# A margin of a moment before a maximum is handed to a busy PSUM bank, in the front of a two-branch attention kernel

## The chip, the cores and the metric

The kernel runs on one core of a Trainium2 chip. The core has five engines that run side by side and meet at semaphores: TensorE (PE, with its weight loader PEld), VectorE (DVE), ScalarE (ACT), GpSimd (POOL) and the queue of SyncE (SP), which issues DMAs. TensorE writes to PSUM banks of 128 x 512 words, and VectorE and ScalarE read them. The metric is the device time of one execution in microseconds; it was 1465.76 us for the kernel before (median of 3 runs, 1465.62 to 1465.98).

## What is computed

One sequence of 2048 rows with 512 columns, x, goes through two attentions, which a gate mixes:

```python
g = sigmoid((x * gate_w).sum(-1))
out = g * A(x) + (1 - g) * B(x)
# A: 32 heads of 16; row i looks at rows i, i-2, ..., i-14 (8 of them, dilated by 2)
# B: 32 heads of 16 queries over ONE head of keys and values
scores = einsum("bhqd,bkd->bhqk", q, k) * 16**-0.5    # 32 x 2048 x 2048
p = softmax(scores); o = einsum("bhqk,bkd->bhqd", p, v)
```

Branch B is the larger one by far: its 32 x 2048 x 2048 scores are made twice, once to find the largest score of each row (the *maxima* below, which the softmax subtracts) and once for the exponentials.

## The kernel before, in words

B's scores are cut in 32 units (4 blocks of 512 queries by 8 groups of 4 heads), each of 16 steps of 128 keys. For the maxima a unit has 64 pieces, one for each of 2 x 2 x 4 blocks of 128 rows and 4 blocks of 512 keys: 2048 in all (`NF`). The pieces are 62 rows deep, so two of them, or one and a piece of other work, run side by side on the upper and the lower half of TensorE's rows. Such a pair of places is called a slot here.

The program is written out by a planner in Python: it keeps a clock for TensorE, ScalarE and VectorE (`clk`), the time at which every PSUM bank is free (`free`), and a list of tasks with due times (`tasks`), and at each slot it decides what the next instructions are. Nothing of that is left at run time: each engine has a fixed order of instructions, and where a bank isn't free yet, the engine waits at its semaphore, with all that is behind it in its queue. The planner counts 0.23 us for a slot (`T_R`), 0.20 for the way from a matmul to its reader (`T_LAT`), 0.66 for a fused add-and-maximum (`T_TTR`), 1.14 and 0.61 for the maximum of a pair and of a single.

There are three stages.

- **The front** (`stream` called with `mm` and `done_mm`, profile lines L1209 for its matmuls): 62 lumps of work, the query projections of B (14) and the query, key and value projections of A (48), each of 12 products that are split in two row halves and add up in the banks `pe`. `stream` hands out one projection matmul per row half and slot. Between them it puts maxima in: in a slot where a maximum goes to one half, the projections go on in the other. In the first part of the front these are whole maxima: `fill_pair` (two matmuls at L387 into bank `pm`, key `m2`; one VectorE reduction at L416) and `fill_one` (one matmul at L387 into `ps` or `po`, keys `m1` and `po`; one reduction at L427).
- In the later part of the front the maxima are taken in *halves*. `half_keys` and `half_parts` form half the sum and half the difference of neighbouring blocks of keys (matmuls at L456 with the matrix `sel`, ScalarE at L464, VectorE at L468, into the tile `kcd`). Then max(a, b) = (a+b)/2 + |a-b|/2: `fill_diff` makes the difference (matmul L483 into a half of `pm`, |.| by ScalarE at L509 into the buffer `dd`), and `fill_sum` the sum (matmul L483 into `ps` for the one row half and `po` for the other, and one VectorE instruction at L526 that adds `dd` and takes the maximum). Two matmuls so give two pieces, but with half of VectorE's work. `diff_ready` and `sum_ready` say whether one may be handed out; `paired` says whether the next two pieces can be taken in halves, among others because the half keys of their blocks are there (`formed`). At most 468 pieces (`FRONT`) are begun in the front in this way.
- **The attention stage** (512 steps): per step two pairs of score matmuls (L571), two exponentials on ScalarE (L573), eight matmuls with the values (L581), and one pair and at times one single of the maxima that are left (L387). Branch A's arithmetic runs beside it on POOL (L645 to L705). Twice an **output phase** (`out_phase`, L865) interrupts it; it calls `stream` too. The list `pe` is empty in the front and not empty from the attention stage on, which is how functions of both tell where they are.

The order around the change is thus set by comparisons of `free[...]` with `clk["pe"]` in `stream`, `sum_ready` and `diff_ready`. Before, a sum, a single or a pair could be handed out when its bank would be free within 0.1 us:

```python
return bool(pend[odd]) and free[("m1", "po")[odd]] <= clk["pe"] + 0.1 and pend[odd][0][2] <= clk["pe"] + 0.4
```

and a difference as soon as its half of `pm` is free. `formed[g]` was set to 0.0 when `half_parts` had been written out.

Of the kernel before, what the change touches and what calls it, by code (L numbers as in the profile page):

```python
# [43 lines left out]
FRONT = 468  # L44
LEAD, M2S, M1S, E1S, PER_ROW = 3.0, 0.5, 0.3, 0.2, 21
M2H = 0.15
WB = 6


# [31 lines left out]
def gated_mix_kernel(ctx, tc, xt, wa, wk, wq, wo_a, wo_b, out):  # L81
# [27 lines left out]
    m1 = pp.tile([P, 512], F32, name="ps")  # L109
    po = pp.tile([P, 512], F32, name="po")  # L110
    m2 = Banks(tc, "pm")

    def split(hi, lo, src, eng=None):
        nc.scalar.activation(hi, src, AF.Copy)
        (eng or nc.vector).tensor_sub(lo, src, hi.bitcast(F32))

    clk = {"pe": 0.0, "act": 0.0, "dve": 0.0}

    def after(eng, ready, dur):
        clk[eng] = max(clk[eng], ready) + dur  # L120
        return clk[eng]
# [15 lines left out]
    raw = [first[:, k, :] for k in range(4)]  # L137
    raw += [p1.tile([P, 512], F32, name="xraw", tag=tag, bufs=WB) for tag in ("wah", "wal") for _ in range(6)]
    xraw = {(t, c): raw[C * t + c] for t in range(NQB) for c in range(C)}
# [16 lines left out]
    def load_wa(gg, c):  # L156
        waraw[gg, c] = p1.tile([P, GN], F32, name="waraw", bufs=2)
        nc.gpsimd.dma_start(waraw[gg, c], wa[c * P:(c + 1) * P, gg * GN:(gg + 1) * GN])

    def split_wa(gg, c):  # L160
        nonlocal pool
        wah[gg, c] = p1.tile([P, GN], F32R, name="wah", bufs=WB)
        wal[gg, c] = p1.tile([P, GN], F32R, name="wal", bufs=WB)
        split(wah[gg, c], wal[gg, c], waraw.pop((gg, c)), nc.gpsimd)
        after("act", clk["pe"], 0.62)
        pool = max(pool, clk["pe"] * 1e3) + 1300

    def ahead_wa(gg, k):

        if 0 <= k < 2 * C and k % 2 == 0:  # L170
            load_wa(gg, k // 2)
        if 2 < k <= (2 * C if gg == 0 else 2 * (WB - C)) + 1 and k % 2:
            split_wa(gg, (k - 3) // 2)
# [188 lines left out]
    slots = [(v, pr, t, kc) for kc in range(2) for v in range(2) for pr in range(2) for t in range(4)]  # L362
# [3 lines left out]
    free = {"m2": 0.0, "m1": 0.0, "e0": 0.0, "e1": 0.0, "po": 0.0}  # L366
# [3 lines left out]
    def fillable():  # L370
        return bool(half) or bool(slots) and slots[0][0] < len(stacked) and stacked[slots[0][0]] <= clk["pe"]
# [17 lines left out]
    def to_go():  # L389
        return 2 * len(slots) + len(half)  # L390
# [41 lines left out]
    sel, kcd, dd, formed, ended, wants = [], [], [], {}, set(), []  # L432
# [15 lines left out]
    def half_keys(g):  # L448

        if g == 0:  # L450
            hb[g] = (m2.shape(2)[:, 0, :], m2[:, 1, :])
        keys = ("m2", "m2") if g == 0 else ("m1", "po")
        clk["pe"] = max(clk["pe"], *(free[k] for k in keys))
        for x in range(2):
            for y in range(2):
                nc.tensor.matmul(hb[g][x], sel[0][:, x * y], kst[:, (2 * g + y) * 512:(2 * g + y + 1) * 512], start=(y == 0), stop=(y == 1))  # L456
        clk["pe"] += 1.2
        for k in keys:
            free[k] = clk["pe"] + 4.0
        tasks.append((clk["pe"] + 1.0, half_parts, (g, keys)))  # L460

    def half_parts(g, keys):
        for x in range(2):
            nc.scalar.activation(kcd[0][:, g, x], hb[g][x], AF.Identity, scale=mk[:, 0:1])  # L464
            at = after("act", clk["pe"], 0.65)
        for x in range(2):
            parts = kcd[0][:, g, x]
            nc.vector.scalar_tensor_tensor(parts, hb[g][x], mk[:, 1:2], parts.bitcast(F32), op0=ALU.mult, op1=ALU.add)  # L468
            free[keys[x]] = after("dve", at + 0.1, 0.7) + 0.1
        tasks.append((clk["dve"] + 1.5, lambda: nc.sync.dma_start(kd[:, g], kcd[0][:, g].bitcast(F32)), ()))  # L470
        formed[g] = 0.0

    def half_back():

# [3 lines left out]
    def paired():  # L478
        return len(slots) > 1 and slots[0][3] % 2 == 0 and formed.get(slots[0][3] // 2, 1e9) <= clk["pe"] and slots[1] == slots[0][:3] + (slots[0][3] + 1,) and fillable()
# [4 lines left out]

    groups, pend, half_free = [], [[], []], [0.0, 0.0]

    def diff_ready(odd):

        if max(half_free) != free["m2"]:
            half_free[:] = [free["m2"]] * 2  # L490
        if half_free[odd] > clk["pe"] or clk["dve"] - 1.6 > clk["pe"]:
            return False
        mine = [g for g in groups if odd in g[2]]
        if not mine and (groups or half or ended or wants or not paired() or not pe and NF - to_go() >= FRONT):
            return False
        d = mine[0][1] if mine else dd[0]
        return all(x[1] is not d for x in pend[odd])

    def fill_diff(odd):
        mine = [g for g in groups if odd in g[2]]  # L500
        if not mine:
            mine = [(slots.pop(0), dd[0], {0, 1})]
            slots.pop(0)
            dd.append(dd.pop(0))
            groups.append(mine[0])
        (v, pr, t, kc), d, todo = mine[0]
        m2.shape(2)
        half_mm(m2[:, odd, :], v, pr, t, kc, 1, odd)
        nc.scalar.activation(d[:, odd], m2[:, odd, :], AF.Abs)  # L509
        half_free[odd] = after("act", clk["pe"] + T_R + T_LAT, 0.54) + 0.1  # L510
        free["m2"] = max(half_free)
        pend[odd].append(((v, pr, t, kc), d, half_free[odd]))
        todo.discard(odd)
        if not todo:
            groups.remove(mine[0])

    def sum_ready(odd):

        return bool(pend[odd]) and free[("m1", "po")[odd]] <= clk["pe"] + 0.1 and pend[odd][0][2] <= clk["pe"] + 0.4

    def fill_sum(odd):
        (v, pr, t, kc), d, ready = pend[odd].pop(0)
        m = unit_tile(v)
        dst, key = ((m1, "m1"), (po, "po"))[odd]
        half_mm(dst, v, pr, t, kc, 0, odd)
        nc.vector.tensor_tensor_reduce(d[:, odd], dst, d[:, odd], 1.0, -FMAX, ALU.add, ALU.max, m[:, odd, pr, t, kc:kc + 1])  # L526
        free[key] = after("dve", max(clk["pe"] + T_R + T_LAT, ready), T_TTR) + 0.08
        filled(v, 2)
# [35 lines left out]
    pe, pexp, exped = [], {}, {}  # L564
# [251 lines left out]
    def stream(seq, mm, done, pooled):  # L816

        at, told = [0, 0], 0
        ended.clear()
        while min(at) < len(seq):  # L820
            lone = {}
            if wants and all(free[k] <= clk["pe"] + 0.1 for k in (("m1", "po") if wants[0] else ("m2",))):
                half_keys(wants.pop(0))
            halves = groups or any(pend) or paired() and not half
            if halves or 1 in wants:
                for b in range(2):
                    if sum_ready(b):
                        lone[b] = lambda b=b: fill_sum(b)
                    elif diff_ready(b):
                        lone[b] = lambda b=b: fill_diff(b)  # L830
                        break
            elif fillable() and free["m1"] <= clk["pe"] + 0.1:
                lone[half[0][4] if half else 0] = lambda: fill_one(m1, "m1")
            elif pooled and fillable() and free["po"] <= clk["pe"] + 0.1:
                lone[half[0][4] if half else 0] = lambda: fill_one(po, "po")
            dur = 0.0
            for b in sorted((0, 1), key=lambda b: b not in lone):
                if b in lone:
                    now = clk["pe"]
                    lone[b]()  # L840
                    clk["pe"] = now
                elif at[b] < len(seq):
                    dur = max(dur, mm(b, seq[at[b]]))
                    at[b] += 1
            after("pe", 0, T_R if lone else dur)
            if not (ended or 0 in wants or halves) and slots and fillable() and free["m2"] <= clk["pe"] + 0.1:
                clk["pe"] = max(clk["pe"], free["m2"])
                fill_pair(m2, "m2")
            while told < min(at):
                told += 1  # L850
                done(seq[told - 1])

    def out_phase(js, n, whole_unit):
# [40 lines left out]
        while groups or any(pend):  # L894
            for b in range(2):
                if sum_ready(b):
                    fill_sum(b)
                elif diff_ready(b):
                    fill_diff(b)
            clk["pe"] += T_R  # L900
# [311 lines left out]
    def done_mm(at):  # L1212
        nonlocal pool
        x, i = at
        lump = lumps[x]
        if lump[0] == "a" and lump[2] == NJ - 1 and lump[1] + 1 < GG and i in (2, 5) and WB - C < 4:
            c = WB - C + (i == 5)
            if c < C:
# [175 lines left out]
```

## Time and profile before

| what | value |
|---|---|
| median of the runs | 1465.76 us |
| the profiled execution | 1465.73 us |
| its span, first to last instruction | 1463.9 us |
| granted TensorE clock | 1.000 |
| busy PE / PEld / DVE / ACT / POOL | 1454.2 / 676.5 / 1191.3 / 1286.7 / 1002.8 us |
| front, first to last projection (L1209) | 26.3 to 268 us |
| first and last difference or sum in the front (L483) | 97.6 and 262.4 us |

In the profile a line as L483 is a line of the kernel; `ps<-kcd,qst` means that the tile `ps` is written from `kcd` and `qst`; x20 counts instructions. PEld is the weight loader, which works ahead of the matmuls, so that an idle time of PEld isn't in full an idle time of the array. Ends of matmuls are modelled, and matmuls overlap, so the busy time of PE doesn't tell how many of them went through; the starts do. A wait is given as "who waited <- what ended it: us in total, times, longest".

### The profile page before, as it was taken

The numbers are of one execution on the slowest core, as the hardware profiler recorded it, in microseconds if no ns is written. First come the engines' busy times: TensorE is split into PE (matmuls) and PEld (weight loads), VectorE is DVE, ScalarE is ACT, GpSimd is POOL, SyncE is SP. The second block draws the span as 40 slices with busy tenths as digits, with TensorE's granted clock in tenths as the row PEclk, the third lists the DMA queues.
The fourth block names the chain that finished last, engine by engine and source line by source line (L and its number), as shares of the span: only waits on it lengthen the run. The fifth ranks groups of instructions, "written<-read, shape, count | busy, mean of one in ns | idle before, by whom it ended". The sixth has DMA issues, their size and how long they took to land.

```text
span 1463.9 us, 29004 instructions
## 1 busy us (share of the span) xinstructions
PE 1454.2 (99%) x10612; PEld 676.5 (46%) x10612; DVE 1191.3 (81%) x1867; ACT 1286.7 (88%) x1629; POOL 1002.8 (69%) x1753
## 2 busy tenths in 40 slices
PE   9999999999999999999999999999999999999998
PEld 5877777533333333333333476333333364333343
DVE  6978889688888888888888888888888888888712
ACT  5658888899999999999999988999999988999986
POOL 7853889778898988988878898798988341011221
PEclk9999999999999999999999999999999999999999
DMA  6753433222121120211202111121120000000110
GB/s 225 210 162 77 147 90 103 74 56 66 42 86 34 54 79 22 71 42 42 72 20 74 42 60 60 42 71 38 46 70 14 12 27 16 12 1 2 29 32 30
DMA packets 75263, 89.80 MB, mean 61 GB/s; under 512 B 56368, under 2 KB 56416, under 8 KB 70896
## 3 DMA queue, kind: packets, MB, share of 16 engines
q1 hardware_dynamic: 68176, 49.00, 11.9%
q0 software_dynamic: 6368, 37.90, 7.7%
q8 instruction: 83, 1.36, 0.4%
q10 hardware_dynamic: 576, 1.05, 0.2%
q14 instruction: 60, 0.49, 0.1%
HBM read 60.03 MB, written 27.35 MB: 60 GB/s over the span
## 4 chain that ended last, share of the span: by engine, by line
PE 96%; DVE 2%; POOL 1%; DMA 1%; issue 0%; ACT 0%; DVEq 0%; POOLq 0%; ACTq 0%
PE po L581 34%; PE pe L571 23%; PE pe L1209 10%; PE pm L387 8%; PE ps L387 6%; PE pe L865 4%; PE pm L483 3%; PE ps L483 2%; PE po L483 2%; PE pm L936 1%; PE pe L211 1%; DVE mx L416 1%; DMA xraw<-xt 1%; DVE mx L427 0%; POOL qlo L257 0%
## 5 line engine op out<-in xcount | busy, mean ns | idle before, releaser
L573 ACT ACTIVATE pexp<-pe 128x1024 f32<-128x1024 f32 x1022 | 987.9, 1023 | 83.2 <-PE pe L571 78.7
L416 DVE TENSOR_REDUCE mx<-pm 128x2 f32<-128x1024 f32 x504 | 617.3, 1225 | 145.2 <-PE pm L387 141.7
L581 PE MATMUL po<-pexp,vst 128*32 128x512 f32 x4096 | 545.5, 605 | 0.8 <-DVE tt L595 0.8
L571 PE MATMUL pe<-qst,kst 64*128 64x512 f32 x1916 | 442.8, 451 | 0.0
L571 PEld LDWEIGHTS pe<-qst,kst 64*128 64x128 f32 x1916 | 180.0, 183 | 473.4 <-ACT pexp L573 466.7
L427 DVE TENSOR_REDUCE mx<-ps 128x1 f32<-128x512 f32 x402 | 273.8, 681 | 0.7 <-PE ps L387 0.7
L387 PE MATMUL pm<-kst,qst 62*128 62x512 f32 x973 | 196.9, 397 | 0.7 <-ACT pexp L573 0.4
L645 POOL TENSOR_TENSOR pr<-aext 128x256 f32<-128x256 f32 x256 | 182.6, 741 | 4.6 <-DMA aext<-ad 4.3
L705 POOL TENSOR_TENSOR oa<-oa,av 128x256 f32<-128x256 f32 x224 | 164.3, 733 | 15.1
L581 PEld LDWEIGHTS po<-pexp,vst 128*32 128x32 f32 x4096 | 80.6, 108 | 168.0 <-issue 158.6
L387 PE MATMUL ps<-kst,qst 62*128 62x512 f32 x394 | 155.5, 395 | 0.2 <-DVE mx L427 0.2
L702 POOL TENSOR_TENSOR av<-aext,lg 128x256 f32<-128x256 f32 x224 | 139.6, 623 | 12.7
L509 ACT ACTIVATE dd<-pm 128x512 f32<-128x512 f32 x182 | 102.4, 605 | 21.1 <-PE pm L483 11.8
L1209 PE MATMUL pe<-wah,xh 64*128 64x512 f32 x376 | 119.2, 397 | 0.0
L1209 PE MATMUL pe<-wah,xl 64*128 64x512 f32 x376 | 118.5, 395 | 0.0
L1209 PE MATMUL pe<-wal,xh 64*128 64x512 f32 x376 | 117.5, 394 | 0.0
L387 PEld LDWEIGHTS pm<-kst,qst 62*128 62x128 f32 x973 | 94.5, 186 | 4.5 <-DVE mx L416 1.6
L651 POOL TENSOR_TENSOR tr<-pr 128x512 f32<-128x512 f32 x64 | 81.7, 1277 | 4.3
L509 ACT ACTIVATE pexp<-pm 128x512 f32<-128x512 f32 x124 | 70.5, 606 | 13.2 <-PE pm L483 8.3
L608 POOL TENSOR_TENSOR rl<-rl,gate_t 128x16 f32<-128x16 f32 x31 | 6.9, 223 | 107.2 <-DVE rl L602 99.7
L651 POOL TENSOR_TENSOR tr<-tr 128x256 f32<-128x256 f32 (+1 forms) x128 | 72.5, 567 | 8.6
L387 PEld LDWEIGHTS ps<-kst,qst 62*128 62x128 f32 x394 | 73.6, 187 | 4.2 <-DVE mx L427 1.1
(215 smaller groups left out, 1972.6 us busy)
## 6 DMA issues: line engine op xcount, KB each, us to landing
aext<-ad POOLq DMA_DIRECT2D x32, 1056.0 KB, 5.6
qst<-qd SPq DMA_DIRECT2D x60, 128.0 KB
ad<-stage SPq DMA_DIRECT2D x32, 240.0 KB
xraw<-xt SPq DMA_DIRECT2D x16, 256.0 KB
qd<-qhi SPq DMA_DIRECT2D x16, 256.0 KB
qd<-qlo SPq DMA_DIRECT2D x16, 256.0 KB
qst<-qd SPq DMA_DIRECT2D x60, 64.0 KB
qst<-ml SPq DMA_DIRECT2D x216, 2.0 KB
```

What stands on the lines that cost most here:

```text
L387: nc.tensor.matmul(dst, qst[home(v)[0]][b:b + 62, pr, t * P:(t + 1) * P], kst[b:b + 62, kc * 512:(kc + 1) * 512], start=True, stop=True)
L416: nc.vector.tensor_reduce(m[:, :, pr, t, kc], dst, AX.X, ALU.max)
L427: nc.vector.tensor_reduce(m[:, odd, pr, t, kc:kc + 1], dst, AX.X, ALU.max)
L509: nc.scalar.activation(d[:, odd], m2[:, odd, :], AF.Abs)
L571: nc.tensor.matmul(bank[:, odd, :], kst[b:b + 64, kt * P:(kt + 1) * P], qst[home(u)[0]][b:b + 64, pr, :], start=True, stop=True)
L573: nc.scalar.activation(e, bank, AF.Exp, scale=SCALE)
L581: nc.tensor.matmul(po[32 * i:32 * i + 32, :], vst[:, kt, :], pexp[s, i // 2][:, i % 2, :], start=(kt == 0), stop=(kt == NJ - 1))
L645: nc.gpsimd.tensor_mul(pr[:, k], q, e[:, o:o + NH, AC:2 * AC])
L651: nc.gpsimd.tensor_add(nx, cur[:, :, 0:n], cur[:, :, n:2 * n])
L702: nc.gpsimd.tensor_mul(av, e[:, o:o + NH, 2 * AC:].rearrange("p j (h d) -> p j h d", d=DH), lg[:, w].unsqueeze(3).to_broadcast([P, NH, AG, ...
L705: nc.gpsimd.tensor_add(ao, ao, av)
L1209: nc.tensor.matmul(front[2 if x == last else x % 2][0][:, b, :], l[h], r[h], start=(i == 0), stop=(i == 3 * C - 1))
```

## The change

Three comparisons of the front and one due time are altered; no instruction is added or taken out, only the order in which the planner writes them.

A constant `JUST` of 0.05 us and a function `just()` come in, which is 0.05 in the front and -0.1 from the attention stage on. Where a maximum was handed out with its bank free within the next 0.1 us, the front now asks that the plan has had the bank free for 0.05 us: in `sum_ready`, for `fill_one` on `ps` and `po`, and for `fill_pair` on `pm`. `diff_ready` asks for 0.05 instead of 0. In the output phases all four stay as they were, since -0.1 gives the old margin (and 0 in `diff_ready`). And `formed[g]` is the planner's VectorE clock after the half keys' last instruction, plus 0.1, instead of 0.0.

```diff
+JUST = 0.05
@@ half_parts
-        formed[g] = 0.0
+        formed[g] = clk["dve"] + 0.1
@@
+    def just():
+        return -0.1 if pe else JUST
@@ diff_ready
-        if half_free[odd] > clk["pe"] or clk["dve"] - 1.6 > clk["pe"]:
+        if half_free[odd] > clk["pe"] - max(0.0, just()) or clk["dve"] - 1.6 > clk["pe"]:
             return False
@@ sum_ready
-        return bool(pend[odd]) and free[("m1", "po")[odd]] <= clk["pe"] + 0.1 and pend[odd][0][2] <= clk["pe"] + 0.4
+        return bool(pend[odd]) and free[("m1", "po")[odd]] <= clk["pe"] - just() and pend[odd][0][2] <= clk["pe"] + 0.4
@@ stream
-            elif fillable() and free["m1"] <= clk["pe"] + 0.1:
+            elif fillable() and free["m1"] <= clk["pe"] - just():
                 lone[half[0][4] if half else 0] = lambda: fill_one(m1, "m1")
-            elif pooled and fillable() and free["po"] <= clk["pe"] + 0.1:
+            elif pooled and fillable() and free["po"] <= clk["pe"] - just():
                 lone[half[0][4] if half else 0] = lambda: fill_one(po, "po")
@@ stream
-            if not (ended or 0 in wants or halves) and slots and fillable() and free["m2"] <= clk["pe"] + 0.1:
+            if not (ended or 0 in wants or halves) and slots and fillable() and free["m2"] <= clk["pe"] - just():
                 clk["pe"] = max(clk["pe"], free["m2"])
                 fill_pair(m2, "m2")
```

## The prediction

> **What bounds the kernel now.** I read the shares of the chain first, then the stages, then the waits inside the stage that the change touches.
>
> ```profile
> PE 96%; DVE 2%; POOL 1%; DMA 1%; issue 0%; ACT 0%; DVEq 0%; POOLq 0%; ACTq 0%
> ```
>
> The chain that ended last lies on TensorE for 96% of the span. TensorE takes its matmuls in the written order, so time is won where one of them waits and everything behind it waits too. The profiled execution took 1465.73 us with a span of 1463.9, that is 1.83 outside the span; the median of the runs, 1465.76, is 0.03 above it. A change within 0.2%, 2.9 us, is about what a measurement can't tell from none.
>
> The stages, with one query each: all instructions, then the projections (L1209) alone, then the maxima in halves (L483) alone, each for 108 to 263 us; columns are window, length, and per engine busy time with its instructions.
>
> ```profile
> 30.00:92.50 62.50, 62.30 (x524) 53.88 (x524) 60.67 (x85) 37.01 (x80) 53.21 (x47) 1.00 0.68 189
> 108.00:263.00 155.00, 155.00 (x1270) 114.79 (x1268) 132.44 (x386) 134.34 (x269) 114.52 (x177) 1.00 0.38 106
> 108.00:263.00 155.00, 153.85 (x914) 110.46 (x912) 1.00 0.38 106
> 108.00:263.00 155.00, 117.14 (x356) 62.28 (x356) 1.00 0.38 106
> ```
>
> The front is the stretch up to 268 us; its second part carries 914 projection matmuls and 356 maxima matmuls. Two matmuls run side by side on the two halves of the rows, so 1270 are 635 slots. What an undisturbed slot takes, the order of time shows (start, length):
>
> ```profile
> 61.58 0.42 PE L1209 MATMUL pe<-xh,wqh 64*128 64x512 f32 x2
> 61.81 0.41 PE L1209 MATMUL pe<-xl,wqh 64*128 64x512 f32 x2
> ...
> 62.74 0.41 PE L1209 MATMUL pe<-xl,wqh 64*128 64x512 f32 x2
> 62.98 0.41 PE L1209 MATMUL pe<-xh,wql 64*128 64x512 f32 x2
> ```
>
> From 61.58 to 62.98 are six slots (the rows cut out begin 0.23 or 0.24 apart too), so one is 1.40 / 6 = 0.233 us. 635 x 0.233 = 148.0 of 155 us: at most 7.0 us of this stretch are matmuls that waited, although busy PE reads 155.00 of 155. Who waited:
>
> ```profile
> PEld ps L483 <- DVE mx L526: 9.2, 35, 0.4
> PEld po L483 <- DVE mx L526: 8.5, 36, 0.4
> PEld pm L483 <- ACT dd L509: 2.9, 14, 0.3
> PEld pe L1209 <- DVE stage L317: 0.3, 1, 0.3
> ```
>
> The weight loader waits 71 times, 17.7 us, for VectorE to read a sum's bank (ps or po). The loader runs ahead of the matmuls, so not all of this is lost. One recurrence of bank ps:
>
> ```profile
> 214.44 0.40 PE L483 MATMUL ps<-kcd,qst 62*128 62x512 f32 x1
> 214.91 0.40 PE L1209 MATMUL pe<-wah,xh 64*128 64x512 f32 x1
> 214.99 0.69 DVE L526 CUSTOM_DVE_ANT_0 dd<-ps,dd 128x512 f32<-128x512 f32 x1
> 215.04 0.18 PEld L483 LDWEIGHTS po<-kcd,qst 62*128 62x128 f32 x1 [0.17 <-DVE mx L526]
> 215.15 0.40 PE L483 MATMUL po<-kcd,qst 62*128 62x512 f32 x1
> 215.39 0.39 PE L1209 MATMUL pe<-wah,xh 64*128 64x512 f32 x1
> 215.60 0.08 DVE L526 DVE_READ_ACCUMULATOR2_ANT mx<- 128x1 f32 x1
> 215.74 0.18 PEld L483 LDWEIGHTS ps<-kcd,qst 62*128 62x128 f32 x1 [0.40 <-DVE mx L526]
> 215.74 0.50 PE L483 MATMUL ps<-kcd,qst 62*128 62x512 f32 x1
> 216.08 0.39 PE L1209 MATMUL pe<-wah,xl 64*128 64x512 f32 x1
> ```
>
> The next sum on ps was due at 215.39 + 0.23 = 215.62, began at 215.74, and the slot after it began 0.34 later instead of 0.23: 0.12 + 0.11 = 0.23 us lost, one slot, with a loader's wait of 0.40. The wait of 0.17 at 215.04 cost nothing: po began at 215.15, 0.24 after its neighbour. So some 0.17 of each wait is covered.
>
> **The change, part by part.** *The margin of the sums, from 0.1 us too early to 0.05 us late (sum_ready).* No instruction is added or removed; some are written later. In the plan's numbers a sum's bank is free 0.23 + 0.20 + 0.66 + 0.08 = 1.17 us after its slot begins. With the old margin the next sum may go when 1.07 have passed, which is the fifth slot (5 x 0.23 = 1.15); with the new one 1.22 must pass, which is the sixth (1.38). The trace says that the bank really needs 215.74 - 214.44 = 1.30 us, and six real slots are 1.40. So a quick recurrence, given out one slot too early now and paid with a lost slot, would find its bank free, and the lost slot would carry a projection. The gain from below: 17.7 - 71 x 0.17 = 5.6 us (waits shorter than their cover count against it). From above: the 7.0 us less what the ScalarE waits lose, 2.9 - 14 x 0.17 = 0.5, so 6.5. I take 5.6, the figure from the waits themselves; at 0.23 each these are 24 recurrences.
>
> *The same margin for the first part's maxima (fill_one, fill_pair).* The reductions of a pair and of a single:
>
> ```profile
> L416 DVE TENSOR_REDUCE mx<-pm 128x2 f32<-128x1024 f32 x504 | 617.3, 1225 | 145.2 <-PE pm L387 141.7
> L427 DVE TENSOR_REDUCE mx<-ps 128x1 f32<-128x512 f32 x402 | 273.8, 681 | 0.7 <-PE ps L387 0.7
> ```
>
> In 30 to 92.5 us VectorE is busy 60.67 of 62.50, and that covers a later issue: with three banks in turn, the two others hold a reduction of a pair and one of a single, 1.23 + 0.68 us of VectorE's work (or two singles, 1.36), while a bank is refilled one slot later. Cost nothing; without the cover it would be 0.23 us a round.
>
> *The first group of a half (diff_ready, 0.05 later).* The plan gives ScalarE's read 0.23 + 0.20 + 0.54 + 0.1 = 1.07 us, the fifth slot lies at 1.15 and so 0.08 behind it: the new margin moves little, and I leave the 0.5 us of those waits where they are.
>
> *Half keys ready when VectorE is through.* Now the first such matmul goes as soon as the work on the keys is written down:
>
> ```profile
> 96.47 0.40 PE L1209 MATMUL pe<-wah,xl 64*128 64x512 f32 x2
> 96.65 0.74 DVE L468 SCALAR_TENSOR_TENSOR kcd<-po,mk,kcd 128x512 fp32r<-128x512 f32 x1
> 97.57 0.18 PEld L483 LDWEIGHTS pm<-kcd,qst 62*128 62x128 f32 x1 [1.13 <-issue]
> 97.60 0.47 PE L483 MATMUL pm<-kcd,qst 62*128 62x512 f32 x1 [0.74 <-PE pe L1209]
> ```
>
> It was due at 96.47 + 0.23 = 96.70 and began at 97.60: 0.90 us lost behind the write of the keys at 96.65 to 97.39. Between nothing (the plan's VectorE clock runs ahead) and 0.90; I take 0.90, since the new due time is that very instruction's. A plain maximum of a pair may slip in before the first group and hold it up by its 1.2 us of VectorE; that moves a few maxima and no projection.
>
> *What comes later for it.* The count of projections is fixed, so the front ends 5.6 + 0.9 = 6.5 us sooner and with fewer maxima. They go at 356 / 155 = 2.3 a us, so 6.5 x 2.3 = 15; the 24 recurrences come 0.10 later each, 1.2 us on either bank, 3 more: 18 maxima move to the attention stage. Each spares half a slot in front, 0.117 us, 2.1 in all. What one costs later, units of 16 steps (32 exps, L573) with different counts of maxima show (all engines, then L573 alone, then L387 alone):
>
> ```profile
> 399.90:433.00 33.10, 33.10 (x238) 11.92 (x234) 27.49 (x34) 31.01 (x33) 29.49 (x49) 1.00 0.29 94
> 1245.60:1279.50 33.90, 33.74 (x242) 12.20 (x241) 29.24 (x34) 31.02 (x33) 0.84 (x2) 1.00 0.04 10
> 399.90:433.00 33.10, 30.92 (x32) 1.00 0.29 94
> 399.90:433.00 33.10, 10.00 (x44) 5.08 (x42) 1.00 0.29 94
> 433.00:466.40 33.40, 11.02 (x47) 5.46 (x45) 1.00 0.05 14
> 1245.60:1279.50 33.90, 11.61 (x48) 5.68 (x47) 1.00 0.04 10
> ```
>
> 0.8 us for four maxima more is 0.20 each, 0.3 for three is 0.10. The floor is nothing (ScalarE, 31.0 of 33 to 34 us, hides it), the ceiling far off a whole matmul's length, 0.395. I take 0.15, between the two pairs: 18 x 0.15 = 2.7. The attention stage's own margins stay as they are. POOL's branch A sets when the second output phase may start:
>
> ```profile
> 1149.74 0.73 POOL L705 TENSOR_TENSOR oa<-oa,av 128x256 f32<-128x256 f32 x1
> 1171.24 0.24 POOL L533 TENSOR_TENSOR mh<-mt,mk 128x32 fp32r<-128x32 f32 x1 [20.67 <-DVE mt L406]
> ```
>
> It is done 20.67 us ahead of the next work on POOL, more than the front can shrink, so that phase keeps its unit; if it didn't, it would begin 34 us later.
>
> **Sum:** -5.6 - 0.9 - 2.1 + 2.7 = -5.9 us. Against the profiled 1465.73 that is 1459.8.
>
> **The rivals.** *A, the forecast:* 1459.8, with its own range from 1456.2 (6.5 + 0.9 + 2.1 and nothing later: 9.5) to 1462.8, where 2.9 is won.
>
> *B, the front isn't paced by TensorE.* In 108 to 263 us ScalarE is busy 134.34 and VectorE 132.44 of 155 us, the weight loader only 114.79. If ScalarE paces, each slot won turns into a wait of a projection for its bank, and only the half keys' 0.9 stays: 1464.8. Against it:
>
> ```profile
> L509 ACT ACTIVATE dd<-pm 128x512 f32<-128x512 f32 x178 | 100.1, 606 | 19.4 <-PE pm L483 10.1 <-PE pe L1209 5.9 <-PE ps L483 2.2
> ```
>
> ScalarE idles 19.4 us ahead of the half maxima, 18.2 of it for TensorE: it follows. The Trainium skill, "Perfetto Trace Analysis", section "Identifying the Most-Contended Engine", would have TensorE judged by the weight loader's busy share and the engine of the highest occupancy optimized first. By that rule ScalarE (87% by the row above) would come first and the change would give B's time; the 635 slots, 95% of the stretch, speak for the sum instead.
>
> *C, the moved maxima cost more than they spare, and it gets slower.* If every one of the 178 sums slips a slot, not 24, then a pair of sums that now takes 155 / 89 = 1.74 us takes 1.97, an eighth fewer maxima: 43, and 15 for the shorter front, 58. At the ceiling of 0.395 each the result is -6.5 + 58 x (0.395 - 0.117) = +9.6, 1475.3. It decides, slower by 2.9, from 0.28 us for each. The sixth-slot recurrences that exist already and the slope of 0.10 to 0.20 speak against it.
>
> *D, the change doesn't do what it says:* the plan's clock and the chip's drift apart, so that the same number of sums meets a busy bank, one slot later. Then gains and losses cancel: 1465.
>
> **How the numbers follow.** A 0.58, B 0.13, D 0.11, C 0.18. The predicted time is A's. Faster 0.58; the same, B and D, 0.24; slower, C, 0.18. The range runs from 1456 over B and D to 1468, where C ends at a price of 0.27; beyond both ends remain some 0.2.
>
> **What would show it.** Right: in the front few waits of about 0.4 us of the loader for L526 in place of 71 waits, 17.7 us; no wait of 1 us ahead of the first L483; the first exp (L573) some 8 us sooner; 346 rather than 364 matmuls of L483 in the front; 18 more of L387 later, at unit lengths of 33.1 to 33.9. Wrong: the number of L526 waits stays; or L1209 begins to wait for ScalarE; or the attention stage, from the first exp to the end, grows by clearly more than 2.7 us.

## The result and the profile after

The changed kernel takes 1461.73 us (median of 9 runs, 1461.16 to 1462.19) against 1465.66 of the kernel before in the same series (1465.19 to 1465.98): ratio 0.9973, 95% interval 0.9963 to 0.9983. It is 3.9 us faster; the forecast was 5.9. The profiled execution has a span of 1460.0 us, 3.9 less than before. (Of two of the experiments below, the margins alone and the first series of sums and differences, the profile is of an execution at a lower granted clock, 0.949 and 0.869; no duration is taken from these two, and the ratio given for the margins alone still has that execution, 1476.52 us, in it, while its median has not moved by it.)

Where the 3.9 us were won is read from the first score matmul of the attention stage (its weight load; columns: shortest, median and longest, first and last start), before and then after:

```profile
L571 PEld LDWEIGHTS pe<-qst,kst x1916: 182/183/188, 265.4 to 1450.1; 64*128 64x128 f32 x192
```

```profile
L575 PEld LDWEIGHTS pe<-qst,kst x1916: 182/183/188, 262.1 to 1446.2; 64*128 64x128 f32 x192
```

The front ends 3.3 us sooner, and the rest, 1460.0 - 262.1 = 1197.9 us, is 0.6 shorter than before (1463.9 - 265.4 = 1198.5). The changed program's lines stand one to four further down: L387 is now L388, L483 L484, L509 L513, L526 L530, L571 L575 and L1209 L1213.

The front's second part after the change, all engines, and then who waited in it on TensorE's side:

```profile
108.00:260.00 152.00, 151.64 (x1280) 115.84 (x1278) 131.63 (x386) 135.05 (x269) 115.29 (x179) 1.00 0.39 106
```

```profile
PEld po L484 <- DVE mx L530: 5.9, 33, 0.5
PEld pm L484 <- ACT dd L513: 5.4, 23, 0.7
PEld ps L484 <- DVE mx L530: 5.3, 32, 0.2
```

640 slots of 0.233 us are 149.1 of 152 us, so 2.9 us are lost to waits, not 7.0 of 155. There are still 65 waits for VectorE ahead of a sum, but they sum to 11.2 us, which is 65 x 0.17: nearly all of it lies under the loader's cover (one wait of 0.5 us for po doesn't). The waits for ScalarE ahead of a difference have grown, from 2.9 us in 14 to 5.4 in 23. One recurrence of bank ps shows it in the order of time:

```profile
224.33 0.39 PE L484 MATMUL ps<-kcd,qst 62*128 62x512 f32 x1
224.87 0.69 DVE L530 CUSTOM_DVE_ANT_0 dd<-ps,dd 128x512 f32<-128x512 f32 x1
225.49 0.08 DVE L530 DVE_READ_ACCUMULATOR2_ANT mx<- 128x1 f32 x1
225.62 0.18 PEld L484 LDWEIGHTS ps<-kcd,qst 62*128 62x128 f32 x1 [0.16 <-DVE mx L530]
225.73 0.39 PE L484 MATMUL ps<-kcd,qst 62*128 62x512 f32 x1
```

From sum to sum are 1.40 us, six slots, and the loader waits 0.16 at no cost. Counted from the starts of the sums in both traces, 27 of them came under 1.37 us after the one before on their bank, and 44 between 1.37 and 1.50; after the change it is none and 84. The forecast's own sign of being wrong, that the number of these waits stays, came all the same (65 of 71): a wait under the cover counts as one too. What tells the two kernels apart is the length: 26 waits of a sum were over 0.3 us before, one is after.

But the place where the half keys had held up the first difference looks different from what was forecast. The first L484 comes at 107.6 us, not at 97.6, and ahead of it a projection waits:

```profile
104.25 1.27 ACT L465 ACTIVATE kcd<-pm,mk 128x512 fp32r<-128x512 f32 x2
104.97 1.41 DVE L469 SCALAR_TENSOR_TENSOR kcd<-pm,mk,kcd 128x512 fp32r<-128x512 f32 x2 [1.66 <-ACT kcd L465]
105.63 0.39 PE L1213 MATMUL pe<-wah,xl 64*128 64x512 f32 x2
106.29 0.68 DVE L318 TENSOR_TENSOR stage<-pe,stage 128x512 f32<-128x512 f32 x1
107.12 0.50 PE L1213 MATMUL pe<-wah,xh 64*128 64x512 f32 x2 [1.10 <-DVE stage L318]
107.57 0.47 PE L484 MATMUL pm<-kcd,qst 62*128 62x512 f32 x1
```

The next projection was due at 105.63 + 0.23 = 105.86 and began at 107.12: 1.26 us lost. VectorE idled 1.66 us in front of the half keys (L469), which wait for ScalarE, and the addition that frees the projection's bank (L318) stood behind them in its queue.

### The profile page after: what moved, and what is told of

Read it like the earlier page. It is cut to its first block, busy times and chain, and to the rows that moved or that the text cites. A ratio compares the mean times of both kernels' runs of the same rounds, so it can differ in the third digit from the quotient of the medians.

```text
span 1460.0 us, 28999 instructions
## 1 busy us (share of the span) xinstructions
PE 1450.1 (99%) x10612; PEld 674.5 (46%) x10612; DVE 1192.3 (82%) x1866; ACT 1285.6 (88%) x1627; POOL 1001.5 (69%) x1753
## 4 chain that ended last, share of the span: by engine, by line
PE 96%; DVE 2%; ACT 0%; POOL 0%; issue 0%; DVEq 0%; POOLq 0%; ACTq 0%
PE po L585 35%; PE pe L575 23%; PE pe L1213 11%; PE pm L388 8%; PE ps L388 6%; PE pe L869 4%; PE pm L484 3%; PE ps L484 2%; PE po L484 1%; PE pm L940 1%; PE pe L212 1%; DVE mx L417 1%; DVE mx L428 0%; PE po L186 0%; DVE tt L599 0%
## 5 line engine op out<-in xcount | busy, mean ns | idle before, releaser
L577 ACT ACTIVATE pexp<-pe 128x1024 f32<-128x1024 f32 x1022 | 987.1, 1022 | 83.1 <-PE pe L575 79.9
L575 PE MATMUL pe<-qst,kst 64*128 64x512 f32 x1916 | 442.2, 451 | 0.0
L575 PEld LDWEIGHTS pe<-qst,kst 64*128 64x128 f32 x1916 | 179.9, 183 | 473.5 <-ACT pexp L577 467.5
L388 PE MATMUL pm<-kst,qst 62*128 62x512 f32 x975 | 196.8, 397 | 0.4 <-ACT pexp L577 0.4
L388 PE MATMUL ps<-kst,qst 62*128 62x512 f32 x396 | 156.0, 394 | 0.2 <-DVE mx L428 0.2
L1213 PE MATMUL pe<-wah,xh 64*128 64x512 f32 x376 | 119.3, 396 | 1.1 <-DVE stage L318 1.1
L1213 PE MATMUL pe<-wah,xl 64*128 64x512 f32 x376 | 119.7, 394 | 0.0
L1213 PE MATMUL pe<-wal,xh 64*128 64x512 f32 x376 | 118.9, 394 | 0.0
L513 ACT ACTIVATE dd<-pm 128x512 f32<-128x512 f32 x180 | 102.1, 606 | 15.2 <-PE pm L484 6.8
L388 PEld LDWEIGHTS pm<-kst,qst 62*128 62x128 f32 x975 | 94.3, 186 | 4.2 <-DVE mx L417 1.1
L513 ACT ACTIVATE pexp<-pm 128x512 f32<-128x512 f32 x124 | 70.5, 605 | 14.4 <-PE pm L484 7.0
L388 PEld LDWEIGHTS ps<-kst,qst 62*128 62x128 f32 x396 | 74.0, 187 | 4.3 <-issue 1.2
```

The lines of the kernel that those rows point to most:

```text
L388: nc.tensor.matmul(dst, qst[home(v)[0]][b:b + 62, pr, t * P:(t + 1) * P], kst[b:b + 62, kc * 512:(kc + 1) * 512], start=True, stop=True)
L575: nc.tensor.matmul(bank[:, odd, :], kst[b:b + 64, kt * P:(kt + 1) * P], qst[home(u)[0]][b:b + 64, pr, :], start=True, stop=True)
L577: nc.scalar.activation(e, bank, AF.Exp, scale=SCALE)
L1213: nc.tensor.matmul(front[2 if x == last else x % 2][0][:, b, :], l[h], r[h], start=(i == 0), stop=(i == 3 * C - 1))
```

## The experiments

The theory after the result: the sums' margin works as the prediction has it, and the rest of the change costs something. The change has five comparisons, not three (in `sum_ready`, in `diff_ready`, and in `stream` for a single on ps, a single on po and a pair), and one due time; the experiments take them apart. All times below are medians of a kernel's own runs; the kernel before had 1465.62, 1465.71 and 1465.68 us in the three series.

### The margins alone, the half keys alone, the sums alone

```diff
# margins only: the changed kernel with
-        formed[g] = clk["dve"] + 0.1
+        formed[g] = 0.0
# keys only: the kernel before with
-        formed[g] = 0.0
+        formed[g] = clk["dve"] + 0.1
# sums only: the kernel before with, in sum_ready,
-free[("m1", "po")[odd]] <= clk["pe"] + 0.1 and
+free[("m1", "po")[odd]] <= clk["pe"] + (0.1 if pe else -0.05) and
```

> The changed kernel with formed[g] = 0.0 as before, so the margins alone. Theory 1 (the margin of the sums carries the gain, and the due time of the half keys gives back what it wins): the waits of the loader for VectorE before sums cost the front under 0.5 us instead of 6.3; the 0.9 us before the first difference is back, and the 1.25 us wait of a projection for bank pe at 107 us is gone. Front 3 to 5 us shorter than before, time 1460 to 1462.5. Rival (the due time of the half keys is what shifts the halves and so wins): the sums' waits stay above 3 us and the time is 1464 or more.

> The kernel before with the half keys' due time alone. Theory 1: the 0.9 us wait before the first difference goes, a new wait of a projection of about 1.2 us comes, the sums' waits keep their 6 us; time 1465 to 1467. Rival (the due time wins): 1463 or less.

> The kernel before with the new margin in sum_ready alone; singles, pairs, differences and the half keys are as before. Theory 1: this one comparison holds all of the gain: sums' waits cost under 0.5 us, time 1459.5 to 1461.5, no slower than the changed kernel. Rival (the margins of singles and pairs, which come ahead of the halves, matter too): 1463 or more.

*Margins only:* 1461.72 us (ratio 0.9983, 0.9967 to 0.9999). It equals the changed kernel to 0.01 us, and VectorE's, ScalarE's and POOL's instructions stand in the same order in both traces (1866, 1627 and 1753 of them), so next to the margins the half keys' due time does nothing. But half of theory 1 fell: in its trace a projection still waits for bank pe ahead of the first difference, which still comes some 10 us late. Late halves thus come from a margin.

*Keys only:* 1467.38 us, ratio 1.0013 (1.0004 to 1.0022), 1.8 us slower. The wait ahead of the first difference is gone, and here the order of time from 95.99 us on says what took its place:

```profile
95.99 0.74 DVE L468 SCALAR_TENSOR_TENSOR kcd<-ps,mk,kcd 128x512 fp32r<-128x512 f32 x1
96.13 0.50 PE L387 MATMUL pm<-kst,qst 62*128 62x512 f32 x2
97.61 0.40 PE L387 MATMUL ps<-kst,qst 62*128 62x512 f32 x1
98.29 0.40 PE L387 MATMUL po<-kst,qst 62*128 62x512 f32 x1
99.56 1.20 PE L456 MATMUL pm<-kst,sel 128*128 128x512 f32 x4
105.13 0.40 PE L483 MATMUL pm<-kcd,qst 62*128 62x512 f32 x1
```

A pair slips in at 96.13; its partner among the pieces is then taken one by one; and by then the other half keys are due (L456), which need bank pm, where differences go. The halves begin at 105.1 instead of 97.6. What this costs stands further on, and it is the kind of wait that the changed kernel has at 107 us:

```profile
116.47 0.39 PE L1209 MATMUL pe<-wal,xh 64*128 64x512 f32 x1
116.68 0.21 DVE L406 STREAM_TRANSPOSE mt<-ms 128x32 f32<-128x32 f32 x1
116.98 0.69 DVE L317 TENSOR_TENSOR stage<-pe,stage 128x512 f32<-128x512 f32 x1
117.82 0.47 PE L1209 MATMUL pe<-wah,xh 64*128 64x512 f32 x1 [0.96 <-DVE stage L317]
```

A projection due at 116.47 + 0.23 = 116.70 begins at 117.82, 1.12 us late, since the addition L317 comes late in VectorE's queue, behind sums and the end of a unit's maxima (L406), though ScalarE's part of the work (L305) was through at 114.41. A new wait of a projection had been expected for this kernel, of 1.2 us. At 208.23 another waits for the same line, 0.72 us late. The two outweigh the 0.90 that was saved; the front ends 1.3 us later (266.7 against 265.4).

*Sums only:* 1464.03 us, ratio 0.9989 (0.9981 to 0.9998), 1.6 faster, so 2.3 of the changed kernel's 3.9 are missing and the expectation of 1459.5 to 1461.5 failed. Its waits on TensorE's side, 96 to 263 us:

```profile
PEld pm L483 <- ACT dd L509: 12.9, 48, 1.4
PEld po L483 <- DVE mx L526: 4.5, 26, 0.3
PEld ps L483 <- DVE mx L526: 3.1, 18, 0.3
```

The sums' waits are down to 7.6 us in 44, under their cover. The waits of differences (bank pm, read by ScalarE) have grown from 2.9 us in 14 to 12.9 in 48. With the sums handed out as their banks allow, the differences became the ones that come too early.

### Fewer maxima in the front

```diff
-FRONT = 468
+FRONT = 428
```

> The changed kernel with FRONT 428 instead of 468, so 40 maxima are moved from the front to the attention stage. The prediction's prices (0.117 us spared, 0.15 paid for each) give +1.3 us against the changed kernel, 1463.0; a price of 0.20 gives +3.3, 1465.0; nothing to pay gives -4.7, 1457.0; a whole matmul's 0.395 gives +11, 1472.9.

1467.37 us, 5.6 more than the changed kernel for 40 maxima moved (40 matmuls fewer of L484 in the front, 320 against 360). Its first score matmul and its span (1465.4 us) give both prices:

```profile
L575 PEld LDWEIGHTS pe<-qst,kst x1916: 182/183/188, 256.8 to 1451.1; 64*128 64x128 f32 x192
```

The front is 262.1 - 256.8 = 5.3 us shorter, 0.13 for each; the attention stage takes 1465.4 - 256.8 = 1208.6 us, 10.7 more, 0.27 for each. The prediction had 0.117 and 0.15: a maximum that is moved costs 0.14 net, not 0.03.

### Sums and differences together; differences without; fills alone

```diff
# sums and differences: the sums-only kernel with, in diff_ready,
-half_free[odd] > clk["pe"] or
+half_free[odd] > clk["pe"] - (0.0 if pe else 0.05) or      # 0.15 in another run
# no difference margin: the changed kernel with
-half_free[odd] > clk["pe"] - max(0.0, just()) or
+half_free[odd] > clk["pe"] or
# fills only: the changed kernel with the old sum_ready, diff_ready and formed[g]
```

> The kernel before with the margin for sums and the 0.05 us for differences; singles, pairs and half keys as before. Theory 2 (with the sums' margin alone the wait passes to the differences, 5.0 us in place of 0.5, and the 0.05 us takes it from there): waits before differences cost 1 to 2 us of the front, those before sums under 0.5, first difference at 97.5 us with its 0.9; no wait of 1.25 for bank pe; time 1459.5 to 1461.5, 3 to 4 us below the margin of the sums alone. Rival (the margins of singles and pairs brought the rest, by moving the start of the halves): about 1464, as with the sums alone.

> The margins for sums and differences alone, a second time, for a profile at the full clock. Expected: 1460 to 1461; first difference at 97.6 us with its 0.9 us, waits before sums under 0.5 us and before differences 1 to 2, no wait of 1.25 for bank pe.

> The same with 0.15 us for differences. Theory 2: at 0.23 us a slot the margin of 0.15 sends most differences a slot later than 0.05 does; their waits go under 0.5 us, but the halves come slower, so that a few of the 468 maxima are left for the attention stage; time within 1 us of the kernel with 0.05. Rival (waits pass on again, to projections or sums): waits stay, the time too.

> The changed kernel without the 0.05 us for differences. Theory 2: waits before differences rise from 1.4 us to about 5, time 1464.5 to 1466. Rival (that margin moves little, as the prediction had it): 1461.5 to 1462.5.

> The kernel before with the new margin for singles and pairs alone. Theory 2: these bring nothing by themselves: first difference at about 107.6 us instead of 97.6, a wait of a projection of about 1.25 us for bank pe near 107, sums' waits still 5 to 6 us; time 1465.5 to 1467.5. Rival (they hold a part of the gain): 1464.5 or less.

*Sums and differences with 0.05:* 1460.37 us in its second series (ratio 0.9963, 0.9950 to 0.9977); the first had 1460.72 (0.9964, 0.9952 to 0.9977). This is 3.7 us better than the sums alone, at the price of nothing but 0.05 us in one comparison, and it is faster than the changed kernel by 1.4 (its slowest run, 1460.54, is under that one's fastest, 1461.16). Its waits from 96 to 263 us:

```profile
PEld pm L483 <- ACT dd L509: 5.7, 24, 0.8
PEld po L483 <- DVE mx L526: 5.3, 32, 0.2
PEld ps L483 <- DVE mx L526: 4.9, 30, 0.2
PEld pm L483 <- issue: 1.1, 1, 1.1
```

The differences' waits are back from 12.9 to 5.7 us, the sums' lie under their cover, and the 1.1 us ahead of the first difference are there as in the kernel before.

*With 0.15:* 1463.70 us (0.9986, 0.9977 to 0.9995). The differences hardly wait any more (1.7 us in 2), but only 444 maxima get into the front: 24 are moved, and the attention stage grows from 1458.8 - 261.0 = 1197.8 to 1461.8 - 258.2 = 1203.6 us, 0.24 for each. I had expected a difference of 1 us, it is 3.3: the price again.

*Without the margin for differences:* 1462.48 us (0.9979, 0.9970 to 0.9988), 0.75 slower than the changed kernel, where 2.8 to 4.3 had been expected; the runs of the two overlap, so it is hardly told from none, and the time lies in the range of the rival, by which this margin moves little. Its differences wait 6.9 us in 29, not 12.9 in 48. So how much of the sums' waits passes on to the differences is no constant. It may depend on how the two banks' turns fall against each other, which differs where the halves start elsewhere; no run shows that, and why it is 12.9 in the one and 6.9 in the other stays open.

*Fills only (singles and pairs):* 1466.15 us (1.0003, 0.9995 to 1.0012), no difference to before that can be told. The first difference comes at 107.7 us and the wait of 1.5 us for bank pe is there, as expected: both come from these margins.

That late start can be followed in what the planner decides. This is what the planner of the changed kernel holds at three moments, cut to what matters (its clock, the next two pieces, a piece left over, when the half keys are formed):

```
95.18  next (1,0,2,3) (1,0,3,2)   left over [(1,0,0,3,1)]   formed {1: 96.34}
97.02  next (1,0,3,2) (1,0,3,3)   left over [(1,0,2,3,1)]   formed {1: 96.34}
98.68  next (1,0,3,2) (1,0,3,3)   left over [(1,0,2,3,1)]   m2 free at 102.68
```

Halves take two neighbouring pieces, the first with an even last number, and only when none is left over. In the kernel before, at the corresponding moment (94.03), the next were (1,0,2,2) and (1,0,2,3) with none left over. With the new margins a single was left without its partner; when it was gone, pm had been given to the other half keys. It is a matter of which piece happens to be next.

### The half keys with the other two, the addition first, a smaller margin

```diff
# all but fills: sums and differences, and
-        formed[g] = 0.0
+        formed[g] = clk["dve"] + 0.1
# addition first: the changed kernel with
     def half_parts(g, keys):
+        settle("add", 0)
# sums early by 0.03: sums and differences, with
-free[("m1", "po")[odd]] <= clk["pe"] + (0.1 if pe else -0.05) and
+free[("m1", "po")[odd]] <= clk["pe"] + (0.1 if pe else 0.03) and
```

> The same with the half keys' new due time. If that due time does what it says (0.9 us saved), 1459.5 to 1460; if, as alone, it lets an ordinary maximum in that takes the bank and shifts the start of the halves to 105 us, 1461.5 to 1463.

> The changed kernel with a pending addition of a projection's two banks (VectorE, L318) written ahead of the half keys' work. Theory: the projection at 107 us waits 1.25 us because that addition stands behind the half keys (L469) in VectorE's queue, which wait for ScalarE; written first, that wait goes and the time falls by about 1.2, to 1460.5. Rival (the bank is late for another reason): 1461.7 and the wait stays.

> The kernel with the margins for sums and differences, but a sum may be handed out up to 0.03 us ahead of its free bank instead of 0.05 behind. By the prediction's slots (a quick recurrence is free at 1.17 us; the fifth slot, 1.15, is refused only if the margin is tighter than 0.02 ahead) the fifth slot is still taken: waits before sums keep 5 to 6 us and the time is 1464 to 1466. Rival (the gain grows evenly with the margin): about half of the waits are gone, 1462 to 1463.

*All but fills:* 1462.58 us (0.9979, 0.9970 to 0.9988), 2.2 slower than without the due time of the half keys. As when alone, the halves start at 105.1 us. So in both kernels with the old margins for singles and pairs the due time loses, 1.8 and 2.2 us, and the projection that is held up by L317 in the keys-only kernel is held up here too (it begins at 117.66).

*Addition first:* 1460.27 us (0.9964, 0.9951 to 0.9976), 1.5 faster than the changed kernel. The place of the lost 1.26 us now reads:

```profile
103.98 0.69 DVE L318 TENSOR_TENSOR stage<-pe,stage 128x512 f32<-128x512 f32 x1 [0.70 <-ACT stage L306]
104.94 1.41 DVE L470 SCALAR_TENSOR_TENSOR kcd<-pm,mk,kcd 128x512 fp32r<-128x512 f32 x2 [0.28 <-ACT kcd L466]
105.58 0.40 PE L1214 MATMUL pe<-wah,xl 64*128 64x512 f32 x2
105.81 0.40 PE L1214 MATMUL pe<-wah,xh 64*128 64x512 f32 x2
```

The addition comes at 103.98 in VectorE's idle time, the half keys start no later than before, and the projections go on at 0.23. That the order in VectorE's queue was the cause of this wait is shown by this. Of the 1.5 us it is 1.26; the waits of differences fell as well, from 5.4 us in 23 to 3.9 in 19.

*Sums early by 0.03:* 1464.61 us (0.9993, 0.9984 to 1.0002), against 1460.37 with 0.05 late. Its waits from 96 to 263 us:

```profile
PEld ps L483 <- DVE mx L526: 7.9, 33, 0.4
PEld po L483 <- DVE mx L526: 6.8, 32, 0.4
PEld pm L483 <- ACT dd L509: 3.5, 18, 0.4
...
PEld pe L1209 <- DVE stage L317: 1.0, 1, 1.0
```

With 14.7 us in 65 waits 14.7 - 65 x 0.17 = 3.7 us are lost, against 18.1 - 72 x 0.17 = 5.9 in the kernel before over this stretch, and of the 27 recurrences under 1.37 us 19 are left. So the time lies in the range of the first expectation (1464 to 1466) and the waits between the two: 0.07 of the 0.15 us of margin, nearly half, took away 8 of 27, and 19 did keep the fifth slot, as the arithmetic has it. The others may have a bank that the plan makes free at another moment, behind other work in VectorE's queue; they were not followed one by one. In time only 1.1 of 5.3 us are won, also because a projection waits 1.0 us here that doesn't in the kernel with 0.05.

The two best kernels of these, sums and differences alone (1460.37) and the changed one with the addition first (1460.27), beat both kernels of the case and can't be told from each other.

## Why the prediction was right, and where not

The time, 1461.7, lies in the range and in A's own (1456.2 to 1462.8), and it is faster by more than 0.2%. Term by term:

| term of the sum | forecast | what the runs showed |
|---|---|---|
| sums' margin | -5.6 | 17.7 us in 71 waits became 11.2 in 65, all but 0.15 of it under the cover: -5.5 as waits; in time -1.6 alone and -5.3 with the differences' margin |
| singles' and pairs' margin | 0 | +0.4 alone, not told from none; +1.35 next to sums and differences (1461.72 with, 1460.37 without); -1.55 next to the sums alone (1462.48 with the half keys' due time, 1464.03 without both) |
| differences' margin | 0 | -3.7 next to the sums' margin alone, -0.75 in the changed kernel; there the waits still cost 5.4 - 23 x 0.17 = 1.5 us instead of 0.5 |
| half keys' due time | -0.9 | 0.0 in the changed kernel, +1.8 alone, +2.2 with the old fills |
| 18 maxima moved | +0.6 | none moved |

**The sums' margin** was right in its mechanism and its size. The slot arithmetic (the fifth slot at 1.15 for a bank that needs 1.30, the sixth at 1.40) is in the trace, though the run with 0.03 shows that it holds for some 19 of 27 recurrences, and the cover of 0.17 us priced the waits well: what is left is 65 x 0.17. But how much of it arrives as time depends on what is changed beside it: 1.6 us in the sums-only kernel, 5.3 with the differences' margin beside it, 3.2 in the changed kernel without that margin (1465.71 - 1462.48).

**The differences.** The step "the new margin moves little, and I leave the 0.5 us of those waits where they are" looked at the waits of before alone. It asked what the 0.05 do there, and not what is late next once the sums no longer wait. In the sums-only kernel that is the difference, with 12.9 us of waits in place of 2.9. The changed kernel has the 0.05 as well, but its differences still lose 1.5 us where the forecast left 0.5.

**The singles and pairs** were costed at nothing with VectorE's work as the cover. That cover held nearly: up to the first half keys 275 slots took 66.4 us before and 278 take 67.5 now, 0.4 us more than 3 slots of 0.233. What failed is that a margin alters not only when a piece goes but which one is next when the halves become possible. The start at 107.6 us and the 1.26 us behind the addition follow from it. That wait, which no term had, is the largest single piece missing from the forecast gain; the run with the addition first is 1.5 us faster.

**The half keys.** The step that took "0.90, since the new due time is that very instruction's" got the wait right and its sequel wrong. The prediction named the pair that may slip in, and let it move "a few maxima and no projection"; in the keys-only run that pair is there at 96.13 us, the halves start 7.5 us later, and the time rises by 1.8. In the changed kernel the due time isn't what holds the halves back, so it does nothing. The wait of 0.9 is gone there (0.2 is left), but with the margins alone it is gone too: the late start removes it.

**The moved maxima.** 18 were to leave the front; its matmuls of halves are 138 + 2 x 69 + 42 + 2 x 21 = 360 by their counts in the trace against 364, and 4 more of L388 make up for them, so 468 as before. The premise that they go at a constant 2.3 a us failed: 358 in 152 us from 108 to 260 are 2.36, and the first part of the front handed out four more. What stayed the same is their share of the matmuls, 356 of 1270 before and 358 of 1280 after, 0.280 both times: maxima go by the slot, and a slot that is no longer lost carries its share of them. (The four that are whole maxima now are why VectorE has 1866 instructions instead of 1867 and ScalarE 1627 instead of 1629; TensorE has 10612 in both.) The price was mis-sized: 0.24 to 0.27 us in the attention stage instead of 0.15, of which it spares 0.12 to 0.13. With 0.27 the forecast's 18 would have cost 2.5 net; that they didn't move is luck for the total.

**The account of the front.** -5.5 (sums), -0.9 (first difference), +1.0 (differences), +1.3 (addition) and +0.4 (first part) are -3.7; the first score matmul says -3.3, and 0.6 us was won behind it, which no term had. That the total lies as near the forecast as it does is in part chance: losses of 1.3 and 1.0 us that weren't forecast stand against maxima that didn't move, which at the measured price would have cost 2.5.

**The rivals.** B, ScalarE as the pace: the slots lost fell from 7.0 to 2.9 us and the front got shorter, so no. The rule of the Trainium skill ("Perfetto Trace Analysis", "Identifying the Most-Contended Engine") that put ScalarE first by its occupancy would, as the prediction used it, have looked for the gain elsewhere; here the trace disagrees, since the waits on TensorE were worth 3.3 us of front with ScalarE's work unchanged (134.34 us busy in 155, then 135.05 in 152). That section names MFU as a second measure for TensorE beside the weight loader's share; the prediction left it out, so it isn't shown that the whole rule would have put ScalarE first. C had its price nearly right (0.28 to decide, 0.24 to 0.27 measured) but not the number, 58; the 0.15 us run shows C at work, where 24 moved maxima take back 3.3 us of 5.3. D didn't come: the sums' waits of 0.4 us are gone, and of what they cost only 1.0 us turned up ahead of the differences.

## What to carry to other kernels

In a queue that is written in advance, a wait costs what it exceeds its cover by; so where time goes in whole slots, as here, a margin that turns a slot too early into the next one was free, while a larger one cost whole slots (0.05 against 0.15 us for the differences: 3.3 us). When a wait is taken away, give the next one in the cycle its margin too, here ScalarE's bank next to VectorE's. And read what a new due time lets through in the meantime, since a planner fills the gap with something, and a bank taken for 1.2 us may be the one that the real work needs. Look also for the addition in VectorE's queue that frees a projection's bank: kernels here lost 0.7 to 1.3 us at one, now at 107, now at 118 or 208 us.

## What was not expected of the hardware

The loader's waits can be read almost as a price list: in this kernel a wait of 0.17 us ahead of a half-row matmul cost nothing and one of 0.40 cost 0.23, a whole slot, half of it in the delayed slot itself and half in the one after (0.34 us to the next start instead of 0.23). Over all waits ahead of L483 from 108 to 263 us in the kernel before: 45 were of 0.15 to 0.19 us, and the median of the starts before and behind them is the undisturbed 0.233; 21 were over 0.36, with 0.357 us from the slot before and 0.337 to the next. So the second half, 0.10 us, falls on a slot that didn't wait itself; the runs don't show why.
